# First chunks in float32, filler products from the start, block products for two groups, and a written order, in a fused scan and gated-MLP kernel

## The chip, the cores and the metric

The kernel runs on one core of a Trainium2 chip. TensorE (PE, with its weight loads PEld), VectorE (DVE), ScalarE (ACT) and GpSimd (POOL) compute; all but a few transfers are issued by SyncE (SP). The metric is the device time in microseconds (us), the median of the runs. Lower is better.

## The reference

For 4 batches, 8 heads, 768 steps and a head width of 48 it computes a decayed linear attention, normalises the rows and applies a gated MLP:

```python
for t in range(S):
    state = alpha[:, :, t, :, None] * state + einsum('bhd,bhe->bhde', k[:, :, t], v[:, :, t])
    y[:, :, t] = einsum('bhd,bhde->bhe', q[:, :, t], state)
x = y.transpose(0, 2, 1, 3).reshape(3072, 384)
xn = x / sqrt(mean(x * x, -1) + 1e-6) * rms_g
out = (silu(xn @ w_gate) * (xn @ w_val)) @ w_out      # 384 -> 1536 -> 384
```

The three weights arrive as float64, which is passed on as 64-bit words.

## The kernel before, in words

**Chunks.** The 3072 rows are 24 chunks of 128 steps (`c0` to `c23`; the first four begin the four batches). `attention` (L679) takes a chunk through: a load (`att`, L418), a running product of the decays in both directions on VectorE (`scan`, L708, with `turn`, L721, between), their products with k and q (`mul_k`, L732; `mul_q`, L744), the scores on TensorE (`scores`, L843), a mask (`masked`, L881), the products with v (`output`, L914), the sums for the next chunk's state (`sums`, L939), the mean square and its power on GpSimd (L980 to L997), the gain (L999 or L1003) and the transposition to `xT`, by TensorE (`x_bring`, L1009) or by a transposing transfer (`x_turn`, L1050).

**Two float16 parts.** Operands are split into a high and a low float16 part, and a product is three products of parts (`SPLIT`, L30). The low part comes from VectorE, or, for the chunks in `LOW_A`, `LOW_K` and `LOW_X`, from a product with minus the identity that takes the high part off in PSUM (`a_less`, L890; `k_less`, L784; `x_less`, L1028) and a ScalarE copy. In the first four chunks the scores are already float32 products (L849); the masked scores and v are split.

**Weights.** `decode` (L508) loads one of 18 blocks of 768 KB (`raw`, two buffers), joins the bits of its 64-bit words into float32 on VectorE (`tail_word` L538 or `tail_bits` L525, sometimes `sign` L530, `join_word` L546 or `join` L557), makes the high part on ScalarE (L563) and the low part on VectorE (`low`, L565). `inspect` (L624) loads each block once more and sums its top bits; `verdict` (L1705) puts all checks together, in the end.

**MLP.** Chunks are taken in groups of 4, 2, 2, 4, 4, 4, 4 (`GROUPS`, L46). For each of 12 blocks f of the inner width, `expert_in` (L1203) makes two times nine products of 128x128 weights with the group's columns (512 or 256 wide, L1220), a Silu (L1231), the gate (L1237) and the two parts of h (L1247, L1251). The first group starts with half its columns for f = 0 to 4 (`EARLY`, `CUTS`). `expert_out` (L1583) makes 36 products of 384 columns for each chunk (L1595). For a group in `FAST`, `fast_out` (L1431) makes seven block products instead of eight (252 products of 192 columns for four chunks, L1475) from sums of h that `mix` (L1284) makes and sums of w_out that `mix_out` (L1370) makes. Only the last group is in `FAST`.

**The order.** Every step is an operation with an engine, a cost, its predecessors and the buffers that it uses (`Plan.op`, L127). `Plan.order` (L139) places them one by one: latest starts are worked out backward from due times, which the tables `PACE`, `GAP`, `LATE`, `NUDGE` and `HOLD` shift, and the ready operation with the earliest one goes next. The result is one fixed program order on each engine and on SP's queue. Buffers are counted in `BUFS` (L61): three PSUM banks `mm` for the MLP, two `raw`, three `att`.

Of the kernel before, what the change touches and what calls it, by code (L numbers as in the profile page):

```python
# [11 lines left out]
I64 = mybir.dt.int64  # L12
AF = mybir.ActivationFunctionType
# [42 lines left out]
TURN_K = [0, 2, 3]  # L56
BANK_M = ["i0", "i1", "i4", "i8", "i10", "o4"]
SIGN_H = ["i0", "i1", "i2", "i4", "i5", "i6", "i7", "i8", "i9", "i10", "i11", "o0"]
LOW_W = ["i6", "o1", "o2"]
# [3 lines left out]
    xT=2, raw=2, wu=2, h16=13, sl=2, h32=3, ob=2, at=3, y=2, mm=3,  # L63
# [3 lines left out]
    ss=0.12, kh2=0.68, scu=1.1, st2=0.34, scan1=0.6, xs=0.5, xh=0.45, xless=0.17, xr=0.46, kid=1.5, kTh=0.65, kTl=0.53, xid=1.3, xTl=0.47, kneg=0.3, kr=0.45,  # L67
    scan=1.16, rec=0.12, kh=0.6, kl=0.6, vl=0.47, ql=0.62, gd=0.12, sd=0.28, sl=0.36, mask=0.59,
    al=0.59, st=0.27, x=0.47, xl=0.53, rest=0.47, sign=0.98, zeroh=0.95, join=0.88, join2=0.47, wl=0.87, claim=0.4, wh2=0.45, ob=0.47,
    dec=0.1, k16=0.62, v16=0.52, q16=0.62, s16=0.36, a16=0.5, sq=0.49, x16=0.53, st0=0.22,  # L70
    wh=0.75, pow=0.65, sc=0.7, sc32=2.02, y=0.57, y0=0.5, y32=1.73, u=0.5, po=1.465,
    sadd=0.36, ts=0.49, tt=0.28, th=0.62, tl=0.49, us=0.35, uo=0.32,
    neg=0.38, wneg=0.2, wl2=0.38,
# [11 lines left out]
PACE = [0.964, 0.85, 1.338, 1.166, 0.85, 1.042, 1.676, 0.954]  # L85
GAP = [0, 24.7, 23.6, -20.3, -16.4, 20.2, -8.0, 94.6]
FIRST_DUE = [0.8, -38.5, -10.6, -40.6]
AHEAD = [-6.7, 14.2, 1.4, 22.2, 13.6, 33.4, 11.7, -52.6]
STRIDE = [11.5, 26.8, 15.0, 31.7, 14.5, 19.7, 12.9, 50.4]
LATE = dict(  # L90
    abs=-241.8, al=13.1, claim=-80.7, gd=30.6, h=76.5, hl=-61.0, join=-40.6, join2=-10.8,
    k16=110.6, kTh=-102.4, kTl=41.8, kh2=33.6, kid=8.5, kl=-66.0, kneg=1.8, kr=-1.1, load=51.7,
    mask=24.4, neg=-24.4, ob=-245.1, po=-69.5, q16=145.3, ql=8.6, rec=-31.9, rest=15.1,
    sadd=18.9, sc=-12.3, scan=36.9, scu=-75.6, sd=-14.3, sign=48.4, sl=-147.4, sq=-42.7,
    ss=-222.7, st=-7.9, st2=6.2, th=1.8, tl=-0.1, ts=10.7, tt=21.4, u=-45.5, uo=-13.4, us=13.8,
    v16=86.1, vl=-20.6, wh=-74.5, wh2=-21.9, wl=-31.4, wneg=-6.0, x=-15.2, x16=158.7, xTl=-6.6,
    xh=36.2, xid=40.4, xl=-209.0, xless=77.7, xr=68.6, xs=8.4, y=-8.3, zero=-99.0,
)
NUDGE = dict(
    al_6=12.9, gd_9=-13.2, kh2_22=5.4, kh2_4=-11.3, kh2_7=-21.8, kh_3=-57.9, kh_4=29.9,  # L100
    mask_12=13.6, mask_5=-27.5, mask_7=-13.1, q16_15=-8.9, q16_9=41.5, ql_7=7.0, rest_i6=29.5,
    rest_i7=38.3, s16_4=-37.2, sc_4=0.7, sc_6=-13.9, sc_7=7.5, scan_10=-2.4, scan_4=33.5,
    scu_20=17.4, st2_15=20.2, st2_5=2.2, st_1=7.0, st_3=34.8, u_2=10.7, u_5=7.9, u_6=3.0,
    u_8=-4.5, vl_16=-18.7, vl_8=36.0, wl_i2=-14.4, wneg_i6=3.0, x_4=8.5, y_10=-5.8, y_13=-5.1,
    y_15=2.7, y_16=7.6, y_4=2.2, y_6=-12.4, y_9=31.6, zeroh_i4=-17.9,
)
HOLD = dict(
    c5=51.4, c7=73.5, i0=19.8, i1=20.2,
)
CHECK_AT = 260.0  # L110
CHECK_STEP = 9.1
CUTS = [0, 2, 4]
SIDE = [3, 1]
FAST = [6]


class Plan:
# [9 lines left out]
    def op(self, engine, cost, fn, deps=(), use=(), due=None, lock=False, kb=0, late=0.0, hold=0.0):  # L127


        o = dict(e=engine, c=cost, fn=fn, d=[d for d in deps if d], u=tuple(use), due=due, lock=lock,  # L130
                 kb=kb, late=late, r=hold, i=len(self.ops), n=[])
        for d in o["d"]:
            d["n"].append(o)
        for k in o["u"]:
            self.users[k] = self.users.get(k, 0) + 1
        self.ops.append(o)
        return o

    def order(self):  # L139
        for o in reversed(self.ops):  # L140
            lat = WAIT.get(o["e"], LOAD_LAG + LOAD_END + 1.5)
            due = [n["s"] - lat for n in o["n"]] + ([o["due"]] if o["due"] is not None else [])
            o["s"] = min(due, default=1e6) - o["c"]
        for o in self.ops:
            o["s"] += o["late"]
        free = {t: [(0.0, i) for i in range(n)] for t, n in BUFS.items()}
        held, left, last = set(), dict(self.users), {}
        engine = dict.fromkeys(("PE", "DVE", "ACT", "POOL", "SP"), 0.0)
        ready = {e: [] for e in engine}
        wait = {o["i"]: len(o["d"]) for o in self.ops}  # L150
        for o in self.ops:
            if not o["d"]:
                ready[o["e"]].append(o)
        bus, port, done = BUS0, 0.0, []

        owner = [None]

        def start(o):
            t = max(engine[o["e"]], o["r"])
            if o["lock"] and t < port and o["e"] != owner[0]:  # L160
                t = port
            want = {}
            for k in o["u"]:
                if k not in held:
                    want[k[0]] = want.get(k[0], 0) + 1
            for tag, n in want.items():
                f = sorted(free[tag])
                if len(f) < n:
                    return None
                t = max(t, f[n - 1][0])  # L170
            return t

        while len(done) < len(self.ops):
            best = None
            for e, ops in ready.items():
                at = [(start(o), o) for o in ops]
                at = [x for x in at if x[0] is not None]
                if not at:
                    continue
                t0 = min(x[0] for x in at)  # L180
                t, o = min((x for x in at if x[0] <= t0 + 0.12), key=lambda x: (x[1]["s"], x[1]["i"]))
                if best is None or t < best[0]:
                    best = (t, o)
            assert best, "the plan is stuck"
            t, o = best
            e = o["e"]
            ready[e].remove(o)
            for k in o["u"]:
                if k not in held:
                    held.add(k)  # L190
                    free[k[0]].sort()
                    self.slot[k] = free[k[0]].pop(0)[1]
            cost = o["c"]
            if o["lock"]:
                port, owner[0] = t + cost, e
# [13 lines left out]
            for n in o["n"]:  # L209
                n["r"] = max(n["r"], t + cost if n["e"] == e else o["f"])  # L210
                wait[n["i"]] -= 1
                if not wait[n["i"]]:
                    ready[n["e"]].append(n)
            done.append(o)
        return sorted(done, key=lambda o: o["t"])
# [126 lines left out]
def tile_attn_moe(  # L342
# [103 lines left out]
    for h, rows in enumerate((slice(HC, P), slice(0, HC))):  # L446
        a0 = S_A[1] / (S_K[h] * S_Q[1])
        nc.gpsimd.memset(mask[rows, :, 0], a0 * S_QP)
        nc.gpsimd.memset(mask[rows, :, 1], a0)
# [12 lines left out]
    for x, scale in ((same, -1.0), (minus_w, 1.0 / S_W), (plus_w, -(2.0**128) / S_W)):  # L462
        nc.scalar.activation(x, minus, AF.Copy, scale=scale)
    eps = const.tile([P, 1], F32, name="eps")
    rare = const.tile([P, 1], F32, name="rare")
    for h, rows in enumerate((slice(0, HC), slice(HC, P))):
        nc.gpsimd.memset(eps[rows], 1e-6 * (S_Y[h] / S_X) ** 2)
        nc.gpsimd.memset(rare[rows], 1e6 * (S_X / S_Y[h]) ** 2)
    junk = const.tile([P, DM], BF16, name="junk")
    mhalf = const.tile([P, 1], F32, name="mhalf")  # L470
    nc.gpsimd.memset(mhalf, -0.5)
# [12 lines left out]
    nc.gpsimd.memset(stat[:, o_qq : o_qq + NB], 2.0**10)  # L484
# [17 lines left out]
    who = [None]  # L502

    def add(engine, kind, *args, **kw):
        late = LATE.get(kind, 0.0) + NUDGE.get(f"{kind}_{who[0]}", 0.0)
        return op(engine, COST[kind], *args, late=late, **kw)

    def decode(src, dst, name):  # L508

        t = {}  # L510
        who[0] = name

        def load():
# [8 lines left out]
            t["lo"], t["hi"] = r32[:, :, 0], r32[:, :, 1]  # L522
            t["hif"] = raw.bitcast(F32).rearrange("p (n two) -> p n two", two=2)[:, :, 1]
# [14 lines left out]
        def tail_word():  # L538
            nc.vector.tensor_scalar(word(), t["lo"], 29, None, op0=ALU.logical_shift_right)

# [61 lines left out]
        o = op("SP", 0.9, load, [], [raw], kb=786, late=LATE["load"], hold=HOLD.get(name, 0.0))  # L602
        if by_half:
            ot = add("DVE", "rest", tail_word, [o], [raw, wu], lock=True)
# [19 lines left out]
    def inspect(src, dst, name, col, hold):  # L624

        t = {}
        who[0] = name

        def load():
# [7 lines left out]
            t["hi"] = raw.bitcast(I32).rearrange("p (n two) -> p n two", two=2)[:, :, 1]  # L637

        def top_bits():
            u = buf(wst, [P, NW], I32, "wu", name)  # L640
            t["u"] = u.bitcast(F32)
            nc.vector.tensor_scalar(u, t["hi"], W_TOP_BITS, None, op0=ALU.bitwise_and)  # L642

        def range_sum():
            c = col - o_w
            nc.scalar.activation(t["u"], t["u"], AF.Copy, accum_out=wsum[:, c : c + 1])  # L646

        def high_sum():
            split_hi(t["u"], dst[:, 0], col)

        raw, wu = ("raw", name), ("wu", name)
        o = op("SP", 0.9, load, [], [raw], kb=786, due=hold + 40, hold=hold)
# [1214 lines left out]
```

## Time and profile before

| | us |
|---|---|
| median of 3 runs | 519.63 (518.57 to 520.5) |
| span of the profiled execution, first to last instruction | 516.0 |
| outside the span, against the median | 3.6 |
| TensorE busy | 496.0 (96%) |
| VectorE busy | 439.9 (85%) |
| ScalarE busy | 289.5 (56%) |
| GpSimd busy | 23.9 (5%) |

A busy time is the sum of the stretches in which the engine had an instruction under way. TensorE's matmuls are pipelined, so the distance from one start to the next is the cost of one, and not its own duration. Float32 products show two records each.

### The profile page before, as it was taken

To read this page: it belongs to the slowest core of one execution; us is meant where nothing else is said; L and a number is where in the kernel's file an instruction comes from. 1 tells how busy PE (TensorE), PEld (TensorE's weight loads), DVE (VectorE), ACT (ScalarE), POOL (GpSimd) and SP (SyncE) were. 2 spreads that over 40 slices of the span, in tenths; PEclk is the share of its full clock that TensorE was granted. 3 is DMA by queue.
4 is the path that set the end of the run, shared out by engine and by line. 5 is a ranking of instruction groups with operands and counts; after the bars stand their busy time and mean duration, and the time that the engine had idled before them with its cause. 6 is when DMAs were issued, how large, how long until landed. Compare 5 with 4: busy or idle time off the path is not lost.

```text
span 516.0 us, 13326 instructions
## 1 busy us (share of the span) xinstructions
PE 496.0 (96%) x5447; PEld 309.3 (60%) x5447; DVE 439.9 (85%) x905; ACT 289.5 (56%) x775; POOL 23.9 (5%) x51
## 2 busy tenths in 40 slices
PE   3878999999999999999999999999999999999996
PEld 2657744667877886444566545456555556544496
DVE  8999999999999999997999999994157769886643
ACT  3689876554556573464545687673267662354320
POOL 2011000010001010000000000000000100000000
PEclk9999999999999999999999999999999999999999
DMA  8957857539314435652757986243612221000001
GB/s 227 298 178 217 246 183 232 184 82 239 71 41 111 104 86 118 136 92 72 165 102 182 254 190 143 69 137 109 213 62 77 77 77 47 32 2 0 1 8 58
DMA packets 66354, 63.56 MB, mean 123 GB/s; under 512 B 34848, under 2 KB 60416, under 8 KB 66288
## 3 DMA queue, kind: packets, MB, share of 16 engines
q1 hardware_dynamic: 66144, 62.57, 46.5%
q8 instruction: 43, 0.70, 0.6%
q14 instruction: 23, 0.19, 0.1%
q10 hardware_dynamic: 144, 0.10, 0.1%
HBM read 49.84 MB, written 4.72 MB: 106 GB/s over the span
## 4 chain that ended last, share of the span: by engine, by line
PE 80%; DVE 13%; DMA 3%; ACT 2%; issue 2%; SPq 0%; DVEq 0%; ACTq 0%
PE mm L1220 48%; PE mm_po L1595 19%; PE y L930 2%; PE at L867 2%; PE y L920 2%; DMA raw_i<-w_val 2%; DVE wu_i L547 1%; PE at L952 1%; DVE dk L717 1%; DMA att<-att 1%; DVE raw_o L531 1%; DVE wg L566 1%; DVE h L1250 1%; PE y_w_Y L1475 1%; PE at_w_Y L1475 1%
## 5 line engine op out<-in xcount | busy, mean ns | idle before, releaser
L1220 PE MATMUL mm<-xT,wg 128*128 128x512 f16 (+1 forms) x1602 | 288.6, 338 | 2.0 <-DVE wg L566 0.6
L1220 PEld LDWEIGHTS <-wg 128*128 128x128 f16 x1602 | 153.9, 98 | 122.9 <-issue 1.8
L1595 PE MATMUL mm_po<-wo,h 128*128 128x384 f16 x720 | 121.1, 326 | 0.5 <-DVE ob L1609 0.3
L1595 PEld LDWEIGHTS <-h 128*128 128x128 f16 x720 | 69.1, 98 | 45.6 <-issue 0.7
L491 ACT ACTIVATE h<-h 128x512 f16<-128x512 f32 (+1 forms) x89 | 48.5, 545 | 56.2 <-DVE h L1237 55.4
L1237 DVE SCALAR_TENSOR_TENSOR h<-mm,sl 128x512 f32<-128x512 f32 (+1 forms) x89 | 51.8, 583 | 22.9 <-PE mm L1220 21.7
L1231 ACT ACTIVATE sl<-mm 128x512 f32<-128x512 f32 (+1 forms) x89 | 45.0, 506 | 26.4 <-PE mm L1220 26.2
L717 DVE TENSOR_TENSOR_SCAN dk<-att,seed 112x520 f32<-112x520 f32 x47 | 58.1, 1235 | 0.4
L1250 DVE TENSOR_TENSOR h<-h,h 128x512 f16<-128x512 f32 (+1 forms) x89 | 50.8, 580 | 7.0 <-ACT h L491 6.9
L997 POOL TENSOR_TENSOR ss<-ss,mhalf 128x1 f32<-128x1 f32 x24 | 19.3, 803 | 401.1 <-DVE ss L987 390.1
L907 ACT CAST a<-at 128x512 f16<-128x512 f32 x48 | 27.3, 584 | 8.7 <-DVE at L888 7.2
L930 PE MATMUL y<-v,a 128*128 128x48 f16 x576 | 27.0, 186 | 0.0
L888 DVE TENSOR_TENSOR at<-at,mask 128x512 f32<-128x512 f32 x40 | 26.3, 690 | 0.1
L646 ACT ACTIVATE wu_s<-wu_s 128x768 f32<-128x768 f32 x18 | 15.2, 842 | 19.2 <-DVE wu_s L642 18.9
L910 DVE TENSOR_TENSOR a<-at,a 128x512 f16<-128x512 f32 x38 | 25.0, 682 | 0.1
L930 PEld LDWEIGHTS <-a 128*128 128x128 f16 x576 | 22.9, 98 | 0.5 <-issue 0.4
L920 PE MATMUL y<-s,q 112*128 112x96 f16 x240 | 22.7, 204 | 0.0
L1609 DVE TENSOR_SCALAR ob<-mm_po 128x384 f32<-128x384 f32 x20 | 11.0, 552 | 12.9 <-PE mm_po L1595 12.7
L981 ACT ACTIVATE junk<-y 128x384 bf16<-128x384 f32 x24 | 11.7, 486 | 14.3 <-DVE x L1001 7.6
L491 ACT ACTIVATE k<-kh 112x512 f16<-112x512 f32 x21 | 13.1, 625 | 9.0 <-DVE kh L740 7.7
L920 PEld LDWEIGHTS <-q 112*128 112x128 f16 x240 | 14.7, 96 | 3.7
L491 ACT ACTIVATION_READ_ACCUMULATOR h<-h 128x1 f32 x89 | 16.8, 189 | 0.0
(187 smaller groups left out, 577.5 us busy)
## 6 DMA issues: line engine op xcount, KB each, us to landing
att<-att SPq DMA_DIRECT2D x22, 675.9 KB, 5.5
v<-vtok SPq DMA_DIRECT2D x24, 192.0 KB, 3.3
raw_i<-w_gate SPq DMA_DIRECT2D x12, 384.0 KB, 3.8
raw_i<-w_val SPq DMA_DIRECT2D x12, 384.0 KB, 4.8
raw_o<-w_out SPq DMA_DIRECT2D x6, 768.0 KB, 4.3
raw_s<-w_gate SPq DMA_DIRECT2D x12, 384.0 KB, 5.9
raw_s<-w_val SPq DMA_DIRECT2D x12, 384.0 KB, 5.9
raw_s<-w_out SPq DMA_DIRECT2D x6, 768.0 KB, 4.5
```

The source lines that it names most:

```text
L491: nc.scalar.activation(dst, src, AF.Copy, scale=scale, accum_out=stat[:rows, col : col + 1])
L717: nc.vector.tensor_tensor_scan(out, x, start.rearrange("r g p c -> r (g p c)"), 0.0, op0=ALU.mult, op1=ALU.add)
L888: nc.vector.tensor_tensor(x, x, mask[:, :, 1:].to_broadcast([P, NP // 2, 2, C]), op=ALU.mult)
L907: nc.scalar.copy(a_tile()[:, j, 0], t["sc"][j])
L910: nc.vector.tensor_tensor(a_tile()[:, j, 1], t["sc"][j], a_tile()[:, j, 0], op=ALU.subtract)
L920: nc.tensor.matmul(yps[:, 2 * p * D : 2 * (p + 1) * D], t["q16"][:, x, p, :], s16_tile()[:, y, p].rearrange("r j e -> r (j e)"), start=p = ...
L930: nc.tensor.matmul(yps[:, (2 * p + j) * D : (2 * p + j + 1) * D], a_tile()[:, j, x, p, :], t["v16"][:, y, p, j, :], start=first and p == 0 ...
L1220: nc.tensor.matmul(ps[:, :n], wg[:, f, x, j, kk, :], xT[:, y, kk, cs], start=i == 0, stop=i == 3 * NK - 1,)
L1231: nc.scalar.activation(t["sl"][:, :n], t[0][:, :n], AF.Silu, scale=1.0 / (S_X * S_W))
L1237: nc.vector.scalar_tensor_tensor(t["h"][:, :n], t[1][:, :n], S_H / (S_X * S_W), t["sl"][:, :n], op0=ALU.mult, op1=ALU.mult,)
L1250: nc.vector.tensor_tensor(h16_of(g, f)[:, 1, cs], t["h"][:, :n], h16_of(g, f)[:, 0, cs], op=ALU.subtract)
L1595: nc.tensor.matmul(t[i, c][:, : c[1] - c[0]], h16_of(g, f)[:, x, ts], wo[:, f // 2, y, f % 2, c[0] : c[1]], start=f == 0 and m == 0, stop= ...
```

## The change

- The first four chunks stay in float32 to the end: the masked scores are written as float32 to SBUF, v is used as loaded (in the buffers of the split v), k is turned by TensorE in all four and copied once; `output` and `sums` make one float32 product where they made three of float16. Their splits of k, v and the scores are gone (`LOW_A` keeps chunk 5; `LOW_K`, `TURN_K` go).
- TensorE starts with eleven products of 512 columns on constants (`WARM`) and has 23 single ones (`FILL`) among its first operations.
- `raw` has four buffers, and the scratch for dynamic transfers is cut to 1024. `inspect` works in place in `raw`, and is tied to steps of groups 4, 5 and 6 (counted from 0).
- `FAST` holds the last two groups, so `mix` and `fast_out` run for the sixth group, too. From the second step of a fast group on, its products follow its last step, or the output of the fast group before.
- The mean of the squares is folded into the gain and GpSimd's step.
- The due times and their tables are gone. `PLACE` gives each of the 1963 operations its place, and `Plan.order` only assigns the buffers.

```diff
-LOW_A = [0, 1, 2, 3, 5]
+LOW_A = [5]
...
-LOW_K = [0, 1, 2, 3]
...
+WARM = 11
+FILL = 23
...
-    xT=2, raw=2, wu=2, h16=13, sl=2, h32=3, ob=2, at=3, y=2, mm=3,
+    xT=2, raw=4, wu=2, h16=13, sl=2, h32=3, ob=2, at=3, y=2, mm=3,
...
-FAST = [6]
+FAST = [5, 6]
+CHECK = [(4, f) for f in range(0, 12, 2)] + [(5, f) for f in range(12) if f % 3] + [(6, f) for f in range(4)]
+PLACE = """
+6 36 2 11 0 1r x 3 3b 1b 12 2s 2r 2o 1s 18 1o 32 1n 5 2n y 1w 1m 1 4 7 9 i 1z d e g j h l n v 10 r z 13 16 1g 1l
...
+        place = [int(x, 36) for x in PLACE.split()]
...
+        done = sorted(self.ops, key=lambda o: place[o["i"]])
...
-        v = buf(ain, [P, DM], F32, "v", cc)
+        v = buf(ap, [P, DM], F32, "v16", cc) if cc < NB else buf(ain, [P, DM], F32, "v", cc)
...
+        def kT_copy():
+            t["kT"] = tl(ap, [P, NP, R], F32, "kT")
+            nc.scalar.activation(
+                t["kT"].rearrange("s p r -> s (p r)"), t["kps"][:, : NP * R], AF.Copy, scale=S_V
+            )
...
-                    t["sc"][j], t["sc"][j], mask[:, :, 0].to_broadcast([P, NP, C]), op=ALU.mult
+                    a_first()[:, j], t["sc"][j], mask[:, :, 0].to_broadcast([P, NP, C]), op=ALU.mult
...
+                    if first:
+                        nc.tensor.matmul(
+                            out_y, a_first()[:, j, p, :], v_first(p, j), start=p == 0 and j == 0,
+                            stop=True, skip_group_check=True,
+                        )
+                        continue
...
-                for m, (x, y) in enumerate(SPLIT):
+                for m, (x, y) in enumerate(SPLIT[: 1 if first else 3]):
...
-        ss = add("DVE", "ss", mean, [sq], [key("ss")])
-        rt = add("POOL", "pow", root, [ss], [key("ss")], lock=True)
+        rt = add("POOL", "pow", root, [sq], [key("ss")], lock=True)
...
+    def busy(key, n):
+        def products():
+            x = buf(ps_mm, [P, 512], F32, *key)
+            for _ in range(n):
+                nc.tensor.matmul(
+                    x, minus, minus[:, :1].to_broadcast([P, 512]), start=True, stop=True,
+                    skip_group_check=True,
+                )
+        return products
+    for n in range(FILL + 1):
+        key = ("mm", ("busy", n))
+        add("PE", "fill" if n else "warm", busy(key, 1 if n else WARM), [], [key])
...
-                mix_out(i, now + 40 + i, [sums_of_w[-1]] + state_ops[NC - 1]["qp"])
+                mix_out(i, [])
...
+            if g - 1 in FAST and f:
+                deps.append(tail[0])
+            if g in FAST and f:
+                deps.append(step)
+            step = expert_in(g, f, c0, c1, deps)
+            if (g, f) in CHECK:
+                i = unchecked.pop(0)
+                sums_of_w.append(inspect(w_src[i], w_dst[i], f"s{i}", o_w + i, step))
...
+        "TRN2", target_bir_lowering=False, num_devices=1, dynamic_dma_scratch_size=1024
```

Read out of `PLACE`, the new order of the steps that the prediction speaks of (numbers are places among the 1963): on TensorE four fillers and the eleven products first, then `scores` of c0 (27), `k_bring` c0 (31), `output` c0 (42, 52), `scores` c1 (54) and c2 (80), `x_bring` c0 (83) and c1 (101), the first MLP product, f = 2 (115), f = 3 (123), `k_bring` and `scores` c3 (130, 136), f = 1 (139), f = 0 (163), `x_bring` c3 (177), f = 4 (180), and f = 0 of the other half (190). On VectorE `low` of weight block i2 stands at 102, of i3 at 118, i1 at 135, i0 at 151, i4 at 176, and the low part of `xT` of c3 at 184. The output of the second group's first chunk takes its h blocks 9 to 11 at 638, and VectorE makes the last of them at 634. The new group-5 output starts at 1717, the last group's at 1897. On SP the loads of i2, i3, i1, i0 stand at 12, 20, 24 and 29, among the loads of c0 to c3.

## Rows read from the trace of the kernel before

**Rows 1.** The page: busy times, and the span in 40 slices.

```profile
PE 496.0 (96%) x5447; PEld 309.3 (60%) x5447; DVE 439.9 (85%) x905; ACT 289.5 (56%) x775; POOL 23.9 (5%) x51
...
PE   3878999999999999999999999999999999999996
...
DVE  8999999999999999997999999994157769886643
```

**Rows 2.** Busy time by stretch, with granted clock, DMA share and GB/s last.

```profile
6.45:12.90 6.45, 4.52 (x25) 3.70 (x26) 6.26 (x10) 2.38 (x8) 0.00 (x0) 1.00 1.04 274
12.90:19.35 6.45, 5.30 (x45) 4.08 (x45) 6.38 (x11) 3.33 (x8) 0.00 (x0) 1.00 1.08 321
19.35:25.80 6.45, 6.19 (x49) 4.54 (x49) 6.45 (x11) 5.04 (x11) 1.19 (x1) 1.00 1.10 276
...
48.25:511.40 463.15, 462.30 (x5072) 283.36 (x5070) 394.62 (x829) 256.80 (x696) 15.66 (x26) 1.00 0.44 113
```

**Rows 3.** Timeline of TensorE, 0 to 55: start, length, what, idle before it.

```profile
7.05 2.02 PE L767 MATMUL mm_k<-same,kh 112*128 112x112 f32 x8 [7.05 <-DVE kh L737]
...
30.13 0.77 PE L930 MATMUL y<-v,a 128*128 128x48 f16 x24
...
32.78 1.15 PE L767 MATMUL mm_k<-same,kh 112*128 112x112 f32 x8
33.85 1.16 PE L849 MATMUL at<-qp,kh 48*128 48x128 f32 x16
35.61 0.39 PE L1220 MATMUL mm<-xT,wg 128*128 128x256 f16 x2 [0.59 <-ACT wg L563]
...
48.25 0.83 PE L1011 MATMUL y<-same,x 128*128 128x128 f32 x6
```

**Rows 4.** Chain that ended last, in order of time, single pieces: start, length.

```profile
52.94 8.97 PE mm L1220 x81
...
135.24 0.69 PE at L867 x32
...
422.69 20.48 PE mm_po L1595 x126
443.17 46.62 PE mm L1220 x216
489.79 1.24 PE at_w_X L1475 x15
...
511.38 0.36 DVE h L1496
```

**Rows 5.** Timeline of VectorE, first microseconds.

```profile
3.04 1.39 DVE L703 TENSOR_TENSOR_SCAN dk<-att,seed 112x260 f32<-112x260 f32 x2 [0.98 <-DMA att<-att]
...
6.21 0.69 DVE L737 TENSOR_TENSOR kh<-att,dk 112x512 f32<-112x512 f32 x1 [0.27 <-DMA att<-att]
6.82 0.69 DVE L747 TENSOR_TENSOR qp<-att,dk 112x512 f32<-112x512 f32 x1
```

**Rows 6.** Groups by line and shape: busy us, mean ns, idle before.

```profile
L717 DVE TENSOR_TENSOR_SCAN dk<-att,seed 112x520 f32<-112x520 f32 x47 | 58.1, 1235 | 0.4
L747 DVE TENSOR_TENSOR qp<-att,dk 112x512 f32<-112x512 f32 x24 | 16.4, 685 | 0.1
L547 DVE SCALAR_TENSOR_TENSOR wu_i<-raw_i,wu_i 128x768 int32<-128x768 int32 x10 | 9.5, 948 | 0.0
L539 DVE TENSOR_SCALAR wu_i<-raw_i 128x768 int32<-128x768 int32 x11 | 6.0, 550 | 0.3 <-issue 0.3
L1237 DVE SCALAR_TENSOR_TENSOR h<-mm,sl 128x256 f32<-128x256 f32 x34 | 14.1, 417 | 0.0
L801 DVE SCALAR_TENSOR_TENSOR v<-v,v 128x384 f16<-128x384 f32 x24 | 13.2, 550 | 0.5 <-ACT v L491 0.4
```

**Rows 7.** DMA issues: count, KB each, median us to landing.

```profile
raw_i<-w_val SPq DMA_DIRECT2D x12, 384.0 KB, 4.8
...
out_dram<-h ACTq DMA_DIRECT2D x1, 96.0 KB, 2.3
```

More of the change, by code (lines that the diff above doesn't have):

```diff
@@ L99 @@
[L99 to L106, printed above, removed]
@@ L125, in __init__, with op @@
         self.slot = {}
-    def op(self, engine, cost, fn, deps=(), use=(), due=None, lock=False, kb=0, late=0.0, hold=0.0):
-        o = dict(e=engine, c=cost, fn=fn, d=[d for d in deps if d], u=tuple(use), due=due, lock=lock,
-                 kb=kb, late=late, r=hold, i=len(self.ops), n=[])
+    def op(self, engine, cost, fn, deps=(), use=(), lock=False, kb=0):
+        o = dict(e=engine, c=cost, fn=fn, d=[d for d in deps if d], u=tuple(use), lock=lock, kb=kb,
+                 r=0.0, i=len(self.ops), n=[])
         for d in o["d"]:
@@ L139, in order @@
     def order(self):
[L140 to L145, printed above, removed]
+        place = [int(x, 36) for x in PLACE.split()]
+        assert len(place) == len(self.ops)
         free = {t: [(0.0, i) for i in range(n)] for t, n in BUFS.items()}
-        held, left, last = set(), dict(self.users), {}
+        left, last = dict(self.users), {}
@@ L148, in order @@
         engine = dict.fromkeys(("PE", "DVE", "ACT", "POOL", "SP"), 0.0)
[L149 to L160, printed above, removed]
+        bus, port, owner, seen = BUS0, 0.0, None, set()
@@ L161, in start @@
+        done = sorted(self.ops, key=lambda o: place[o["i"]])
+        for o in done:
+            e, cost = o["e"], o["c"]
+            assert all(d["i"] in seen for d in o["d"]), "the order breaks a dependence"
+            seen.add(o["i"])
+            t = max(engine[e], o["r"])
+            if o["lock"] and t < port and e != owner:
                 t = port
-            want = {}
             for k in o["u"]:
-                if k not in held:
-                    want[k[0]] = want.get(k[0], 0) + 1
@@ L166, in start @@
[L166 to L190, printed above, removed]
+                if k not in self.slot:
@@ L210, in order @@
                 n["r"] = max(n["r"], t + cost if n["e"] == e else o["f"])
[L211 to L215, printed above, removed]
+        return done
 def general(tc, pools, seq, w_gate, w_val, w_out, rms_col, out):
@@ L601, in decode @@
         raw, wu = ("raw", name), ("wu", name)
-        o = op("SP", 0.9, load, [], [raw], kb=786, late=LATE["load"], hold=HOLD.get(name, 0.0))
+        o = op("SP", 0.9, load, [], [raw], kb=786)
         if by_half:
-            ot = add("DVE", "rest", tail_word, [o], [raw, wu], lock=True)
+            if name in REST_A:
+                ot = add("ACT", "resta", tail_half, [o], [raw, wu])
+            else:
+                ot = add("DVE", "rest", tail_word, [o], [raw, wu], lock=True)
             os = add("ACT", "zeroh", sign_half, [ot], [raw, wu])
@@ L1282, in tile_attn_moe, with mix @@
     mixed = {}
-    def mix(g, i, end):
+    def mix(g, i):
         (te, he, he_k, e_k, e_hi, e_lo), (to, ho, ho_k, o_k, o_hi, o_lo) = (
@@ L1515, in pe @@
             use += [t_key(i) for i in range(i0, i1) if b in T_AT]
-            tail[0] = done[c, m] = op("PE", cost, lambda: mul(c, m, i0, i1), deps, use, due=now)
+            tail[0] = done[c, m] = op("PE", cost, lambda: mul(c, m, i0, i1), deps, use)
             if i1 < NPR:
@@ L1632, in expert_out @@
                 use = [bank(i, c) for i in range(n)] + [("h16", (g, f)) for f in fs]
-                now += step
-                tail[0] = op("PE", cost, part, [tail[0]] + deps, use, due=now)
+                tail[0] = op("PE", cost, part, [tail[0]] + deps, use)
             for i in range(n):
                 o = ("ob", f"{g}_{t0 + i}")
-                e = add("DVE", "ob", lambda i=i, c=c: back(i, c), [tail[0]], [bank(i, c), o], due=now + 2)
+                e = add("DVE", "ob", lambda i=i, c=c: back(i, c), [tail[0]], [bank(i, c), o])
                 q = ("ACT", 0.1) if c[0] else ("SP", 0.4)
-                op(*q, lambda i=i, c=c: store(i, c), [e], [o], due=now + 5, kb=0 if c[0] else 196)
-        return now
+                op(*q, lambda i=i, c=c: store(i, c), [e], [o], kb=0 if c[0] else 196)
     place, starts = {}, []
@@ L1701, in tile_attn_moe @@
             chunks = [starts[g] + t0 + i for i in range(n)]
-            now = expert_out(g, chunks, t0, now)
+            expert_out(g, chunks, t0)
             t0 += n
+    assert not unchecked
     def verdict():
```

376 lines of the change are left out of this document (197 added, 179 removed).

## The prediction

> **What bounds the kernel now.** I read the busy times first: TensorE is busy 96% of the span, VectorE 85%, and VectorE's slices stand at nine tenths for the first three quarters [rows 1]. Then the stretches. From 48.25 to the last product TensorE is busy 462.3 of 463.15 us [rows 2]; what it idles in the whole program lies ahead of that. So the program is a start of 48 us, then 463 us of packed products, then 4.6 us of eviction, store and end behind 511.36, where the last eviction begins [rows 4]. It can get shorter by fewer columns, or by a shorter start.
>
> The start is bound by VectorE. It begins at 3.04, when the first transfer has landed [rows 5], and is busy 6.38 and 6.45 of 6.45 us in two of its stretches [rows 2]. TensorE is not short of time there but slow: the same eight records of the transposition of k take 2.02 us at 7.05 and 1.15 at 32.78 [rows 3]. By these durations it runs at the lower of its two levels (1.2 GHz) in the first 26 us, although the clock column reads 1.00 throughout, and although the engine is busy for 6.19 of 6.45 us just before [rows 2].
>
> **Prices.** Successive VectorE starts lie 0.08 closer than the lengths (0.69 long, 0.61 apart [rows 5]), so I take every mean less 0.08 [rows 6]: 1.155 for a scan, 0.605 for 512 columns, 0.87 and 0.47 for a 768-column step with two inputs or one, 0.335 for 256 columns, 0.47 for 384. On TensorE nine products of 256 columns take 1.0 (8.97 for 81), nine of 512 columns 1.94 (46.62 for 216), nine of 384 columns 1.46 (20.48 for 126), one block product of 192 columns 0.083 (1.24 for 15) [rows 4].
>
> **Block products for the sixth group.** 144 products of 384 columns at 0.163 go (23.4 us), 252 of 192 columns at 0.083 come (20.8): 2.6 us less on TensorE, where nothing else is free. VectorE gets six more `mix` rounds; per pair two low parts of 512 columns (1.2) become low parts and sums worth about 4, together some 17 us more. It does this in a stretch in which it has slack, since the scans are done by then: nothing, as long as VectorE isn't behind. The last pair's operands are covered by the first step of group 6 (3.9 us) and the three 0:5 parts (3.7 us). If that cover fails, each microsecond goes straight on the end.
>
> **Float32 first chunks.** Gone are, per chunk, both ScalarE copies of the high and of the low scores, two products with minus the identity, and the split of v on ScalarE and VectorE; TensorE turns k in all four chunks (one more at 1.07, the distance between the starts at 32.78 and 33.85 [rows 3]). The float32 products with v don't stand in the trace. Twenty-four float16 ones take at most 0.77 [rows 3]; eight float32 ones cost between that and eight times the 0.28 of one float32 product of 128 columns (0.83 for three, the start at 48.25 [rows 3]), 2.2. They have 48 columns and not 128, so I take 0.8, near the lower end. Over four chunks the ends are 0 and 6 us, but before place 115 TensorE waits for VectorE, so little of that is paid.
>
> **The start, step by step.** VectorE's queue up to the low part of `xT` of c3 (place 184) holds: seven scans and two halves, 9.4; twelve two-input weight steps, 10.4; six one-input ones, 2.8; sixteen steps of 512 columns, 9.7; six of 384, 3.0; four of 256, 1.3; small ones, 1.4. That is 38.0, and with the start at 3.04 and a wait of 0.27 [rows 5] it ends at 41.3. `low` of i4 (place 176) ends 1.6 before, at 39.7; behind it TensorE makes f = 4, two nines of 256 columns, to about 42. I put the start of f = 0 for the other half at 42.5. The other weights come earlier: by the same count i2's low part ends near 23.5, i3's at 26.7, i1's at 31.6, i0's at 35.5, and TensorE has what stands between them done in each gap, if it runs at the higher level.
>
> At 42.5 all of the first half (ten nines) is done. Before, at 48.92, behind `x_bring` of c3, eight nines were (72 records of 256 columns), and two of the four state sums were still to come (about 0.5 each). So the packed stretch begins 6.4 us earlier and holds 3.0 us less: 9.4. With the 2.6 of the block products TensorE's own account is **12.0 us** less.
>
> **Where VectorE takes some of it back.** TensorE now runs ahead of a VectorE that was full already. Up to the last low part of h for the first output of the second group (place 634) its queue holds: 19 scans and two halves, 23.3; 36 two-input weight steps, 31.3; 18 one-input ones, 8.5; 62 of 512 columns, 37.5; ten halves of `mul_k`, 3.4; 27 of 384 columns, 13.1; 44 of 256, 14.5; small ones about 9.5. The sum is 141.1, so it ends at 144.4 at the earliest. TensorE would be there at 42.5 + 34 nines of 256 columns (34) + 14 of 512 (27.2) + 19 of 384 (27.8) + about 12 for scores (0.69 each [rows 4]), outputs and sums = 143.5. VectorE is 1.1 late with no idle at all; I give it 1.9 more for waits in its written order, so TensorE loses 3. Behind that place its lead grows, since weights are done.
>
> **Fillers, buffers, checks.** Eleven and four products of 512 columns at the lower level take about 6.5 us, to 8.4; the first scores could start at 7.5, so up to 0.9 is lost, but VectorE has c1's scans to do meanwhile. Nineteen more at 0.22 (4.1 us) stand in TensorE's waits. Four raw buffers let the loads of i2, i3, i1 and i0 go out before any is used up; SP then issues six transfers of 384 KB ahead of c3's load. The 18 checks move into groups 4 to 6, where ScalarE and VectorE have room; a load lands in about 5 us [rows 7], and the last is issued some 8 us of products before its turn. If it is late, VectorE stands still in the last group. The final check product now stands behind the last product; its three small steps end some 0.6 later than the last eviction, beside a store of 2.3 [rows 7]: between 0 and 0.7, I take 0.3.
>
> **The sum.** 12.0 - 3.0 - 0.3 = 8.7 less than the profiled span of 516.0, that is 507.3; with the 3.6 outside the span, 510.9 against the median of 519.63. The profiled execution is one of the kind that the median stands for, so I subtract from both alike.
>
> **A rule that speaks against the fillers.** The time at the lower level covers at most the first 26 us, in which TensorE is busy for 16 us (4.52, 5.30 and 6.19 [rows 2]); at the higher level that would be 8 less, mostly beside a full VectorE. The Trainium skill (TensorE: Matmul & The Clock Gate, Part 1) holds that the ramp penalty is under 1% of a typical kernel's span. By that figure, and only as an estimate, the fillers could give back at most 5 us; the trace here shows 8 us of products' time, above it. The sum doesn't use either number: it goes by VectorE's queue.
>
> **Rivals.** *VectorE is not late* (0.24): the order has its waits where they cost nothing, so TensorE's account stands, up to 12 less: 507 to 508. For it: VectorE's lateness above is small. Against: VectorE was already without slack in that stretch.
>
> *The start is given back* (0.10): the weights or c3's load land late in the fixed order, VectorE stands still behind an unfinished load, and everything behind it waits. For it: the transfers' share is already above 1.0 at 274 to 321 GB/s [rows 2], and by c3's scan (place 112) some 6 MB are asked for, 20 us at that rate, against a turn at about 25. Late by 5 to 8, it gives 516 to 519: little or no change.
>
> *The clock doesn't hold* (0.07, slower): the change doesn't do what the fillers are there for. The kernel's small and float32 products left the level low for 12 us of nearly unbroken work [rows 2, 3]; if 0.2 us of filler here and there don't hold it, the 27 us of products between 8.4 and 42.5 take up to twice that. As 3 us of idle time absorb the first part, it decides from about 12 us of such work: at 12 the time is as before, at 27 it is 510.9 + 24, near 530; I price it at 523.
>
> **How the numbers follow.** The forecast has 0.59, at 510.9, with 507.5 to 514.5 for its own unknowns (1.9 of VectorE waits may be 0 or 5; the float32 products 0 or 2). Faster by over 0.5% (below 517.0; about what a measurement of this kernel can tell from no change) are the forecast, the first rival and a part of the second: 0.87. No change 0.06, slower 0.07. The range takes in the first rival with a slightly earlier start, 505.5, and the second's near end, 516.5.
>
> **What would show it.** Right: eight records of the transposition of k near 1.1 from the first on; VectorE without idle from 6 to about 140; f = 0 of the second half starting at 42 to 44; TensorE idle by 1 to 4 us between there and 145, and next to nothing later; 252 more records of 192 columns at 0.083. Wrong: products of the first 40 us at twice the length; waits of VectorE for `raw` or `att` transfers; or TensorE waiting in the last two groups, which I take to be free.

## The result, and the profile after

The kernel after takes 510.5 us (median of 4 runs, 509.74 to 510.61), the kernel before 519.1 beside it (4 runs): a ratio of 0.9836, 95% interval 0.9815 to 0.9857. The forecast was 510.9. In the later groups of runs the kernel before had medians of 517.96 to 518.38 (7 to 19 runs). The kernel after was not timed again beside them; if it kept its 510.5, the gain is nearer 8 us than 9. The profiled execution took 510.61, with a span of 508.9.

The page of the kernel after, the lines that answer to [rows 1], with the clock's:

```profile
PE 497.2 (98%) x5490; PEld 319.6 (63%) x5490; DVE 444.0 (87%) x918; ACT 280.3 (55%) x772; POOL 34.6 (7%) x79
...
PE   8999999999999999999999999999999999999994
...
DVE  7999999999999999999999989998999992366742
...
PEclk9999999999999999999999999999999999999998
```

TensorE's thin first slices are filled, and VectorE is full for some five slices longer. Busy time by stretch, answering to [rows 2]; behind the POOL pair stand granted clock, DMA share and GB/s:

```profile
12.00:18.00 6.00, 6.00 (x87) 4.84 (x80) 5.65 (x10) 1.55 (x5) 1.78 (x3) 1.00 1.09 355
18.00:24.00 6.00, 6.00 (x98) 5.46 (x88) 5.58 (x11) 3.66 (x8) 0.91 (x3) 1.00 1.07 312
...
44.60:145.00 100.40, 99.19 (x1088) 67.30 (x1087) 99.50 (x194) 62.64 (x169) 4.02 (x7) 1.00 0.55 156
...
44.60:502.24 457.64, 455.90 (x5060) 287.46 (x5058) 402.37 (x849) 258.04 (x722) 24.52 (x46) 1.00 0.43 112
```

From 44.6 on TensorE idles 1.7 us, of which 1.2 ahead of 145; before it was 0.85 from 48.25 on. VectorE is busy 99.5 of 100.4 us up to 145. TensorE's timeline, answering to [rows 3] (start, length, what, records, idle before it):

```profile
1.73 5.89 PE L1657 MATMUL mm_busy<-minus 128*128 128x512 f16 x15 [1.73 <-POOL minus L444]
...
9.18 1.15 PE L778 MATMUL mm_k<-same,kh 112*128 112x112 f32 x8
...
19.28 1.90 PE L933 MATMUL y<-v,a 128*128 128x48 f32 x16
21.11 1.16 PE L845 MATMUL at<-qp,kh 48*128 48x128 f32 x16
...
42.66 4.09 PE L1216 MATMUL mm<-xT,wg 128*128 128x256 f16 x36
```

The transposition of k takes 1.15 from its first time on. The last row holds f = 4 and then f = 0 of the second half, which so starts at 42.66 + 1.95 = 44.6. The chain that ended last, answering to [rows 4] (start, length):

```profile
438.14 42.73 PE mm L1216 x198
480.88 1.24 PE at_w_X L1477 x15
...
500.74 1.50 PE mm_w_Z L1477 x18
```

The prices are those of before (1.94 for nine products of 512 columns, 0.083 for a block product), and the last block product ends at 502.24 instead of 511.36. VectorE's timeline, answering to [rows 5]:

```profile
2.97 0.92 DVE L714 TENSOR_TENSOR_SCAN dk<-att,seed 112x260 f32<-112x260 f32 x1 [0.91 <-DMA att<-att]
4.49 0.70 DVE L714 TENSOR_TENSOR_SCAN dk<-att,seed 112x260 f32<-112x260 f32 x1 [0.59 <-DMA att<-att]
...
16.48 0.69 DVE L879 TENSOR_TENSOR a<-at,mask 128x512 f32<-128x512 f32 x1 [0.28 <-PE at L845]
...
22.30 1.29 DVE L879 TENSOR_TENSOR a<-at,mask 128x512 f32<-128x512 f32 x2 [0.42 <-PE at L845]
...
43.64 0.55 DVE L1022 TENSOR_TENSOR xT<-y,xT 128x384 f16<-128x384 f32 x1
...
50.05 0.56 DVE L542 TENSOR_SCALAR wu_i<-raw_i 128x768 int32<-128x768 int32 x1
...
146.04 0.76 DVE L1246 TENSOR_TENSOR h<-h,h 128x256 f16<-128x256 f32 x2
```

The row at 43.64 is place 184, the second half of the one at 146.04 is place 634; the one at 50.05 begins a weight block, without a wait for its load. Of the groups of [rows 6] the scan is as it was; the block products' weight loads are twice those of before (504 against 252), one for each product. Of [rows 7] the load of a w_val block takes 2.4 us longer:

```profile
L728 DVE TENSOR_TENSOR_SCAN dk<-att,seed 112x520 f32<-112x520 f32 x47 | 58.0, 1235 | 0.4
...
L1477 PEld LDWEIGHTS <-h 128*128 128x128 f16 x288 | 23.9, 98 | 0.9 <-issue 0.4
L1477 PEld LDWEIGHTS <-att_X 128*128 128x128 f16 x216 | 18.0, 98 | 0.7 <-issue 0.7
```

```profile
raw_i<-w_val SPq DMA_DIRECT2D x12, 384.0 KB, 7.2
```

### The profile page after: what moved, and what is told of

It reads as the page before. It is cut to its first block, busy times and chain, and to the rows that moved or that the text cites. A ratio compares the mean times of both kernels' runs of the same rounds, so it can differ in the third digit from the quotient of the medians.

```text
span 508.9 us, 13442 instructions
## 1 busy us (share of the span) xinstructions
PE 497.2 (98%) x5490; PEld 319.6 (63%) x5490; DVE 444.0 (87%) x918; ACT 280.3 (55%) x772; POOL 34.6 (7%) x79
## 4 chain that ended last, share of the span: by engine, by line
PE 87%; DVE 9%; issue 1%; DMA 0%; DVEq 0%
PE mm L1216 53%; PE mm_po L1593 15%; PE at L863 2%; PE y L939 2%; PE y L922 2%; PE mm_w_Z L1477 2%; PE at L957 2%; PE mm_w_Y L1477 1%; PE y L933 1%; PE at L845 1%; PE mm_w_X L1477 1%; PE at_w_Y L1477 1%; PE y_w_Y L1477 1%; DVE h L1246 1%; DVE raw_o L534 1%
## 5 line engine op out<-in xcount | busy, mean ns | idle before, releaser
L1593 PE MATMUL mm_po<-wo,h 128*128 128x384 f16 x576 | 98.7, 326 | 1.1 <-DVE ob L1607 0.9
L1593 PEld LDWEIGHTS <-h 128*128 128x128 f16 x576 | 54.9, 98 | 37.5 <-issue 1.6
L992 POOL TENSOR_TENSOR ss<-ssq,eps 128x1 f32<-128x1 f32 x24 | 12.8, 535 | 367.6 <-ACT junk L986 367.6
L906 ACT CAST a<-at 128x512 f16<-128x512 f32 x40 | 22.9, 578 | 8.3 <-DVE at L884 8.1
L1477 PEld LDWEIGHTS <-h 128*128 128x128 f16 x288 | 23.9, 98 | 0.9 <-issue 0.4
L497 ACT ACTIVATE q<-qp 112x512 f16<-112x512 f32 x20 | 12.5, 627 | 20.1 <-PE y L922 13.8
L939 PE MATMUL y<-v,a 128*128 128x48 f16 x480 | 23.5, 184 | 0.0
L655 ACT ACTIVATE raw_s<-raw_s 128x768 f32<-128x768 f32 x18 | 16.4, 912 | 8.6 <-DVE raw_s L651 5.4
L497 ACT ACTIVATE att_X<-dk_hs 128x512 f16<-128x512 f32 (+1 forms) x24 | 12.4, 516 | 13.0 <-DVE dk_hs L1313 7.7
L1034 ACT ACTIVATE x<-x,ss 128x384 f16<-128x384 f32 x21 | 12.8, 611 | 12.1 <-POOL ss L993 5.1
L939 PEld LDWEIGHTS <-a 128*128 128x128 f16 x480 | 19.4, 96 | 0.0
```

Source lines behind the costliest of these rows:

```text
L497: nc.scalar.activation(dst, src, AF.Copy, scale=scale, accum_out=stat[:rows, col : col + 1])
L939: nc.tensor.matmul(out_y, a_tile()[:, j, x, p, :], t["v16"][:, y, p, j, :], start=False, stop=m == 2, skip_group_check=True,)
L1477: nc.tensor.matmul(out, left(a, i, x, c), right(b, i, y), start=m in LAST and i == 0 and n == 0, stop=i == NPR - 1 and n == 2, skip_group_ ...
L1593: nc.tensor.matmul(t[i, c][:, : c[1] - c[0]], h16_of(g, f)[:, x, ts], wo[:, f // 2, y, f % 2, c[0] : c[1]], start=f == 0 and m == 0, stop= ...
```

## The experiments

The medians of the kernel before are 518.34 beside the first four, 517.96 beside the next four, 518.38 and 518.12 beside the last two groups. Costs below are differences from the 510.5 of the kernel after, which was timed in the first group only; taken from each group's own ratio they come out between 0.4 us smaller and 1.4 larger.

**What are the fillers worth?** Without any of them, in the new order:

```diff
-            x = buf(ps_mm, [P, 512], F32, *key)
-            for _ in range(n):
+            x = None
+            for _ in range(0):
```

> The changed kernel without the eleven and the 23 filler products; all else, the order too, as it is. Theory: in the start TensorE's products are on the way of VectorE's queue, so at the lower level (the same eight records of the transposition of k at about 2.0 us and not 1.1) VectorE waits for scores and outputs, and the time is 4 to 9 us longer, 514 to 519. Rival one: VectorE's queue alone sets the start, and the fillers are worth less than 1.5 us: 510 to 512. Rival two: all of the change's gain is the clock: back to 519 or above.

Measured: 519.87 (ratio 1.0029, 1.0013 to 1.0045): the whole gain is gone. TensorE's timeline of that run, then its stretches:

```profile
9.65 2.05 PE L778 MATMUL mm_k<-same,kh 112*128 112x112 f32 x8
...
35.02 3.49 PE L933 MATMUL y<-v,a 128*128 128x48 f32 x16
38.31 4.78 PE L1216 MATMUL mm<-xT,wg 128*128 128x256 f16 x27
42.92 1.04 PE L778 MATMUL mm_k<-same,kh 112*128 112x112 f32 x8
```

```profile
12.00:18.00 6.00, 5.67 (x54) 5.58 (x55) 3.77 (x6) 1.24 (x4) 0.00 (x0) 1.00 1.09 354
18.00:24.00 6.00, 5.60 (x59) 5.03 (x59) 3.26 (x7) 1.87 (x4) 1.93 (x3) 1.00 1.07 321
24.00:30.00 6.00, 6.00 (x36) 5.68 (x36) 1.93 (x4) 1.95 (x5) 0.76 (x2) 1.00 0.94 274
```

Records of one kind last twice as long up to about 40 us (2.05 against 1.04), which is the lower of the two levels (1.2 GHz), although TensorE is busy 5.6 to 6.0 of each 6 us and the clock column reads 1.00. VectorE falls to 1.9 busy of 6: in this order TensorE bounds the start as soon as it is slow. The Trainium skill (TensorE: Matmul & The Clock Gate, Part 1) puts the ramp penalty under 1% of a typical kernel's span; here 9.4 of 510.5 us, 1.8%, go with the fillers, and the measurement decides.

**Do the first fifteen do it alone?** The nineteen single ones go:

```diff
+            if key[1][1] not in (0, 2, 4, 7, 19):
+                return
```

> The changed kernel with the fifteen products at its beginning and without the 19 single ones among the first products. Theory: the level, once up, is held by the chunks' own products (TensorE is busy for nine tenths of the start), so nothing is lost, 509.5 to 511. Rival: the small and float32 products let the level fall again, as they left it low in the kernel before; then records of 1.1 us turn to 2.0 somewhere before 28 us, and the time is 2 to 8 us longer.

Measured: 513.13, but spread from 509.66 to 515.84 (ratio 0.988, 0.982 to 0.994, not told apart from the 0.9836 of the kernel after). Two stretches of the profiled execution, with the clock third from the end:

```profile
6.00:12.00 6.00, 4.99 (x68) 3.66 (x66) 5.81 (x10) 0.96 (x3) 0.00 (x0) 1.00 1.05 292
...
18.00:24.00 6.00, 5.75 (x53) 5.66 (x53) 4.59 (x9) 1.82 (x3) 0.25 (x1) 0.50 1.07 277
```

The level falls again at about 13 us, behind a stretch in which TensorE idled 1 of 6 us, and is back at 30. It need not: two executions of this kernel have a mean granted clock of 0.981 and take 515.3 and 515.8, the other two 0.996 and 0.995 and take 511.0 and 509.7. In the four of the kernel after, with the single fillers, it is 0.996 to 0.998.

**Is a warm clock worth as much to the kernel before?** The fifteen products ahead of its first step:

```diff
+    x = ps_mm.tile([P, 512], F32, tag="mm0", name="busy", bufs=1)
+    for _ in range(15):
+        nc.tensor.matmul(
+            x, minus, minus[:, :1].to_broadcast([P, 512]), start=True, stop=True,
+            skip_group_check=True,
+        )
```

> The kernel before with fifteen products of 512 columns on constants ahead of everything, and nothing else. Theory: TensorE is at the higher level from about 8 us on, but VectorE's queue was full from 6 on and stays as long as it was, so the gain is at most 2.5 us: 516.5 to 519. Rival: the slow products were what the start waited for, and the gain is 5 to 8: 511 to 514.

Measured: 518.33, ratio 0.9997 (0.9985 to 1.0009): nothing. A row of TensorE's timeline, and a stretch:

```profile
14.39 1.19 PE L898 MATMUL at<-a,minus 128*128 128x512 f16 x2 [4.47 <-ACT a L914]
```

```profile
18.00:24.00 6.00, 5.74 (x45) 4.31 (x46) 6.00 (x11) 4.77 (x10) 1.19 (x1) 0.50 1.06 249
```

TensorE waits 4.5 us for the split of the scores, the level falls behind it (0.50), and VectorE is full in any case. So fifteen products ahead are worth nothing to the kernel before, and all the fillers 9.4 us to the kernel after. As the level did not last here, no run shows what a lasting one would be worth to the kernel before.

**Are the block products worth their 2.6 us by themselves?** The kernel before, with

```diff
-FAST = [6]
+FAST = [5, 6]
```

> The kernel before with block products for the sixth group, too; the planner makes its order anew with the old tables. Theory: TensorE has 2.6 us less work, and VectorE has room for the sums in the last groups; 516 to 517.5, if the old tables don't put the sums late. Rival: the sums and the buffers of the last groups (two raw, three att) make TensorE wait, and the gain is gone or turned: 519 or more.

Measured: 547.44, ratio 1.0568 (1.0541 to 1.0595). TensorE's waits, and a stretch:

```profile
PE mm_w_Y L1475 <- ACT raw_T L491: 8.2, 3, 3.3
...
PE y L930 <- DVE a L910: 6.0, 2, 4.0
```

```profile
410.00:440.00 30.00, 14.66 (x177) 8.94 (x175) 27.70 (x61) 18.33 (x50) 1.28 (x2) 0.71 0.20 48
```

The tables of the old planner bring the sums of w_out and the last chunks' scores too late; TensorE stands for half of these 30 us and the clock falls to 0.71. With this order fewer columns are no gain; in the written one TensorE waits 0.5 us there.

**Does TensorE's time in the start reach the end?** The float32 products with v made twice:

```diff
-                        nc.tensor.matmul(
...
+                        for n in range(2):
+                            nc.tensor.matmul(
...
```

> The changed kernel with each float32 product of the first chunks with v made twice (64 more records at about 0.11 us, 7 us of TensorE in the start; y of these chunks comes out doubled). Theory: VectorE's queue leads in the start, and TensorE has small gaps there only, so 2 to 5 of the 7 us reach the end: 512.5 to 515.5. Rival one: TensorE is the bound of the start: all 7, 517. Rival two: it is hidden: 510 to 511.

Measured: 518.32, ratio 1.0013 (0.9998 to 1.0029), above what I expected and as rival one had it. The last block product in the chain:

```profile
507.21 1.50 PE mm_w_Z L1478 x18
```

It ends 6.4 us later (508.7), so of the 4 x 1.83 = 7.3 us of products nearly all arrives. **And does less of it help?** One product of 192 columns for four of 48:

```diff
+            if first:
+                nc.tensor.matmul(
+                    yps[:, 4 * h * D : 4 * (h + 1) * D], a_first()[:, 0, 2 * h, :],
+                    tiles["v", cc][:, 4 * h * D : 4 * (h + 1) * D], start=h == 0, stop=True,
+                    skip_group_check=True,
+                )
+                return
...
```

> The kernel after with one float32 product of 192 columns with v per half of a first chunk instead of four of 48 (the output of the first chunks is then another: three of four head products are left out). Four products of 48 columns took 0.92 us; one of 192 should take 0.35 to 0.45 by its columns, so TensorE is freed of 8 x 0.5 = 4 us in the first 44 us. Theory: in the kernel after both engines arrive at 143 us almost together (TensorE lost only 0.8 us to late VectorE steps because it was itself 2.1 us later than forecast), so that VectorE's queue keeps its time and takes the 4 us back as waits of the expert products for the gate: time 509.5 to 510.8, waits for the gate of 2 to 4 us. Rival: VectorE has a lead and TensorE alone sets the time up to 143 us: 506 to 507.5 and no such waits.

Measured: 510.65 (508.94 to 511.0; ratio 0.9843, 0.9825 to 0.986): no gain. TensorE's timeline, its waits for the gate, a stretch, and VectorE's timeline:

```profile
17.88 0.83 PE L921 MATMUL y<-v,a 128*128 128x192 f32 x4
18.71 1.16 PE L845 MATMUL at<-qp,kh 48*128 48x128 f32 x16
...
40.59 4.09 PE L1223 MATMUL mm<-xT,wg 128*128 128x256 f16 x36
...
55.01 5.36 PE L1223 MATMUL mm<-xT,wg 128*128 128x256 f16 x32 [1.20 <-DVE h L1240]
```

```profile
PE mm L1223 <- DVE h L1240: 1.5, 2, 1.2
```

```profile
44.60:145.00 100.40, 97.76 (x1070) 65.54 (x1069) 97.83 (x191) 60.80 (x165) 4.25 (x8) 1.00 0.55 152
```

```profile
41.74 0.56 DVE L1029 TENSOR_TENSOR xT<-y,xT 128x384 f16<-128x384 f32 x1
...
49.92 0.56 DVE L542 TENSOR_SCALAR wu_i<-raw_i 128x768 int32<-128x768 int32 x1 [1.67 <-DMA raw_i<-w_val]
...
145.93 0.76 DVE L1253 TENSOR_TENSOR h<-h,h 128x256 f16<-128x256 f32 x2
```

A chunk's products with v now take 0.83 instead of 1.83, f = 0 of the second half starts at 42.5 instead of 44.6, and place 184 on VectorE ends at 42.2 instead of 44.1. Then a weight load takes the gain back. VectorE waits 1.67 for a w_val block until 49.92, where the kernel after starts the same step at 50.05 without a wait, and TensorE waits 1.20 for the gate behind it. The half of the block that it waits for landed 7.5 us after its issue at 42.3, in the kernel after 5.6 after 44.2: near 49.8 both times. Behind the load VectorE is 0.13 ahead, and it is no more at place 634, which ends at 146.7 where it ended at 146.8; TensorE idles 2.6 us up to 145 instead of 1.2.

So the time is the one that I expected, for another reason: I had looked for 2 to 4 us of waits for the gate, since VectorE's queue keeps its time, and there are 1.5, most of it behind a load. More TensorE work in the start is paid nearly in full; less of it brought nothing, in the profiled execution for a load that came late. Whether the other executions lose it there too, and whether VectorE's own queue would have taken it further on, no run shows.

**How much room has VectorE?** Nine extra steps (3.8 us by their lengths; 0.42 each, where I had taken 0.335) in one place, at 104, 560 or 900 of the order, and then spread over nine places from 700 to 1020:

```diff
...
+            if n == 104:
+                for _ in range(9):
+                    nc.vector.tensor_tensor(extra, flat, flat, op=ALU.mult)
```

> The changed kernel with nine more VectorE steps of 256 columns (0.335 us each, 3.0 us) at place 104, ahead of the first MLP product. Theory: VectorE's queue sets the start, so the end moves by 2 to 3 us: 512.5 to 513.5. Rival: TensorE is the bound by now, and VectorE has that much slack: under 1.

> The same nine VectorE steps at place 560, in the products of the second group (some 130 us into the program). By the prediction VectorE is 1.1 late there, so 2 to 3 us reach the end. What the trace after says: TensorE has no wait between 108 and 430, so VectorE has some slack; then 0 to 1.5 of the 3 us arrive.

> The same nine VectorE steps at place 900, in the fourth group (some 200 us in). Both theories: VectorE's lead has grown behind the last weight, under 0.7 us arrives. If 2 us or more do, VectorE's queue still binds in the middle of the program, and the account of the prediction is wrong.

> The kernel after with the same nine extra VectorE steps (3.8 us by their durations) as in the run with a burst at place 900, but one of them at every fortieth place from 700 to 1020, behind 145 us. The burst there cost 4.2 us, with 3.5 us of waits of the expert products for the gate. Theory: behind 145 us VectorE has free time, and the burst cost only because the three accumulation banks that TensorE can fill ahead hold less than 3 us; spread out, the steps cost 0 to 0.7 us: 510.3 to 511.2. Rival: VectorE has no free time there either, and the steps cost 3 to 4 us wherever they stand: 513.5 to 514.7.

Measured: 514.68, 514.84 and 514.75 for the bursts (ratios 0.9935, 0.9941, 0.9931, each within 0.0018), 511.39 spread out (510.7 to 511.59; ratio 0.9873, 0.9857 to 0.989). The burst at 900, waits and stretches:

```profile
PE mm L1216 <- DVE h L1233: 3.5, 2, 3.0
```

```profile
205.00:212.00 7.00, 3.97 (x18) 1.68 (x17) 6.73 (x18) 2.45 (x9) 0.00 (x0) 0.96 0.60 131
212.00:220.00 8.00, 8.00 (x32) 3.33 (x31) 6.37 (x14) 4.83 (x15) 0.00 (x0) 0.82 0.22 72
```

I had expected slack at 900, and written that 2 us or more would make the account of the prediction wrong. A burst is paid in full there too: TensorE stands 3 us for the gate, and behind that the granted clock is 0.82 for 8 us. (Its profile, of the longest of the four executions, has a second wait for a load, 1.17 us at 50.6, so not all that it is longer comes from the burst.) Spread out, the same work behind 145 us costs 0.9 at the median, just above what the theory gave it, or 1.9 by the ratios; its profile shows no wait for the gate, and its last block product ends at 501.8, 0.4 earlier than in the kernel after. So VectorE has room behind 145 us, but not 4 us at a stretch. Whether the 0.9 are all real the spread of the runs leaves open. As a burst costs as much at 900 as at 560, the one at 560 doesn't show that VectorE is late there.

**Can VectorE be relieved?** The multiplication of q in the first ten chunks on GpSimd:

```diff
+            eng = nc.gpsimd if cc in range(10) else nc.vector
```

> The kernel after with the multiplication of q by its decay in the first ten chunks on GpSimd instead of VectorE: VectorE gives up 4 x 0.68 us before 44.6 us and 6 x 0.69 us from there to 145 us. No row has this step on GpSimd; its scaling of 384 columns took 1.18 us, so 1.2 to 2 us are supposed. Theory: VectorE's queue sets the first 44 us, so the second half's f = 0 starts 1.5 to 2.7 us earlier and the time is 508 to 509.5. Rival: the scores of the first chunks then wait for GpSimd (0.5 to 1.3 us in each), or GpSimd's step slows VectorE's, and it is 510.5 to 515.

Measured: 512.67, ratio 0.9885 (0.987 to 0.9901), slower than the kernel after, as the rival had it. GpSimd's step, and VectorE behind it:

```profile
L759 POOL TENSOR_TENSOR qp<-att,dk x10: 1179/1396/1757, 6.9 to 145.3; 112x512 f32<-112x512 f32 x10
```

```profile
8.66 1.24 DVE L728 TENSOR_TENSOR_SCAN dk<-att,seed 112x520 f32<-112x520 f32 x1 [1.07 <-POOL qp L759]
```

A step of 0.68 becomes one of 1.4 on the way to the scores, and VectorE's scan for the next chunk waits 1.07 for it, so VectorE gains little of what it gave up.

**The tail.** The last check's product and its small steps ahead of the last block product:

```diff
+        pok, flag = self.ops[-2], self.ops[-1]
+        done.remove(pok)
+        done.remove(flag)
+        pe = max(n for n, o in enumerate(done) if o["e"] == "PE")
+        done[pe:pe] = [pok, flag]
```

> The kernel after with the last check's product and its VectorE steps ahead of the last block product. Theory: after the last product the last output's sum and store run in any case, so the time moves by 0 to -0.5 us, though the span's tail falls from 6.7 us to 4.6. Rival: the flag's chain of four steps and a store is what ends last, and the time falls by 1 to 2 us.

Measured: 510.12 (509.51 to 510.61; ratio 0.9842, 0.9828 to 0.9856), the lowest median of all, but not told apart from the kernel after. The span's end stands 6.2 behind the last block product instead of 6.7, and not at 4.6. In the other profiles of the new order, where the end of the program is untouched, it stands 6.9 to 7.8 behind, so these 0.4 are within what it varies by.

## Why the prediction was right, and where its terms were off

**The bound.** Right: the start sets the time, and behind it TensorE is full.

**Block products.** Nothing speaks against the 2.6: the prices are unchanged and TensorE waits 0.5 in that output. But no run takes them out of the written order, and the cover that I named is the order's: with the old tables they cost 29 us.

**Float32 products with v.** This term failed. I took 0.8 a chunk, near the lower end, because they have 48 columns and not 128; sixteen records take 1.83, near the upper end of 2.2. And I held that little of it is paid, since TensorE waits for VectorE there. With them doubled nearly all of it was paid, and with 0.83 instead f = 0 of the second half starts 2.1 earlier: the waiting goes the other way round, masks on VectorE wait for scores that stand behind these products (0.28 and 0.42 in the timeline above).

**The start.** Place 184 ends at 44.1 instead of 41.3: 1.3 of waits (0.27 counted), and 39.8 of steps where I had counted 38.0. Of the waits 0.59 is for c0's second half, which lands late in this profile: three other runs with the same start have f = 0 of the second half at 43.9 to 44.2. Here it starts at 44.6 and not at 42.5, outside the 42 to 44 that I had named as a sign, and TensorE's account is 48.92 - 44.6 + 3.0 + 2.6 = 9.9 less, not 12.0.

**Fillers.** I put the nineteen single ones into TensorE's waits. Eight of them run between 12 and 24, where TensorE has none (6.00 busy of each 6 us). They seem to cost little even so: the two executions without them in which the level lasted took 511.0 and 509.7.

**What VectorE takes back.** The moment was right, the wait that I named did not occur. I had VectorE at place 634 at 144.4 plus 1.9 of waits, 146.3; it was 146.8. TensorE's two waits between 44.6 and 145, and its products at place 638:

```profile
103.87 2.92 PE L1593 MATMUL mm_po<-wo,h 128*128 128x384 f16 x17 [0.19 <-DVE wo L574]
107.72 4.55 PE L1593 MATMUL mm_po<-wo,h 128*128 128x384 f16 x27 [0.93 <-DVE ob L1607]
...
146.89 0.56 PE L957 MATMUL at<-v,kT 64*64 64x48 f16 x48
147.38 5.86 PE L1593 MATMUL mm_po<-wo,h 128*128 128x384 f16 x35
```

It comes to place 638 without a wait, as it was itself 2.1 late; what it idles on the way is for an eviction and a weight of the first outputs. From 44.6 on it lost 0.9 more than before (1.74 against 0.85), and not 3.0. The two errors, 2.1 of start and 2.1 of waits, cancel: the last product should have ended 9.0 earlier and ended 9.1 earlier. Had TensorE come earlier, VectorE, which has next to no idle time up to 146.8, would have held it as I forecast; that is argued, and not shown, since in the one run in which it started earlier a load came between.

**The end.** Here I lost 1.7: the span ends 6.66 behind the last block product against 4.64 before, 2.0 more where I took 0.3. The check's product is not shown to be the reason: moved ahead, it left 6.2. The cause is open: no run tried the order of the last stores, of which SP issues seven from 499.7 on, nor the smaller scratch.

**Outside the span.** It hid that error. I put 3.6 there, against the median; nearly every execution whose time and span are both known shows 1.7 to 1.9, those of the kernel before too (517.84 with a span of 516.0). So the profiled execution of before took, by estimate, 517.8, 1.8 less than the median it was set against. Between the two executions the gain is 7.1, not 8.7; 510.9 was met with 1.6 too little span and 1.9 too much beside it. That it came within 0.4 of the median is luck.

**The rivals.** *VectorE is not late*: not decided. TensorE did not wait for VectorE at place 634, but it was not there early either, and the wide product, whose 4 us brought nothing, lost them at a load. *The start given back by loads*: in the kernel after w_val blocks land 2.4 later, but VectorE waits for none; in the start it waits for c0's two halves alone (0.91 and 0.59). It is close even so: in the profiles of three other runs VectorE waits 0.7 to 1.7 for one near 50. *The clock doesn't hold*: it holds, but the mechanism is real and decides: without the singles it fell in the profiled execution and, by the times, not in every one; and without any filler the time is that of before. (The upper end of that rival's reckoning was added up wrong: 510.9 + 24 is 535, not near 530.)

## What to carry to other kernels

Where less work on a full engine brings nothing, look in that very run for the wait that took the gain, before naming the other full engine: here it was a weight load. A burst of work on an engine with room costs what it costs on a full one, if what is filled ahead of it is shorter than the burst. At a program's start judge TensorE's level by the durations of equal records and not by its busy share or the clock's column, and count a wait of some microseconds in dense products twice: once itself, once in the slower products behind it. Set a profiled span against its own execution's time.

## What the runs showed of the hardware

- Without fillers the lower level lasted some 40 us under nearly unbroken products, most of 48 to 128 columns in float32; with 34 products of 512 columns among them, 11.3 us in all, the first records already ran at the higher one. The clock column prints 1.00 for such a stretch at the program's start, and 0.50 in the two profiles in which the level had been high before.
- Behind waits for VectorE of about 3 us in the middle of dense products the granted clock was 0.82 for 8 us (the burst at 900).
- Eight float32 products of 48 columns took 1.83 (0.23 each), two of 192 columns 0.83 (0.42 each): four times the columns for less than twice the time.
- The second half of a weight block, 384 KB, landed near 49.8 in the kernel after, 5.6 us behind its issue, and in the run with wide products, 7.5 behind its own; the DMA share from 45 to 50 us was 1.00 (293 GB/s) and 1.05 (258 GB/s).
- GpSimd took 1.18 to 1.76 us for a product of 512 columns that VectorE makes in 0.68.
